# Moving the scaling of dO, the first class sorts and four short weight loads in a fused forward and backward kernel

## Chip, cores and metric

One core of one Trainium2 chip runs the whole program. The metric is the device time of one launch in microseconds; three runs of the kernel before gave 1368.88, 1370.08 and 1371.35 us, with a median of 1370.08 us. All other times come from one profiled execution, which took 1368.51 us; its span from the first to the last instruction is 1366.7 us, so 1.8 us lie around it.

## What is computed

The forward pass mixes two branches by a gate, and the program returns the output and the gradients of seven inputs:

```python
def _A_ref(x, w_r, w_i):                      # spectral branch
    X = rfft2(x.astype(float32), axes=(-2, -1)) * (w_r + 1j * w_i)
    return irfft2(X, s=(S, D)).astype(bfloat16)
def _B_ref(x, w_gate, w_up, w_down):          # GEGLU branch
    return (gelu(x @ w_gate) * (x @ w_up)) @ w_down
g = sigmoid((x * gate_w).sum(-1, keepdims=True))
out = g * _A_ref(x, ...) + (1 - g) * _B_ref(B_x, ...)
# vjp with grad_out = dO, for A_x, A_w_r, A_w_i, B_w_gate, B_w_up, B_w_down, gate_w
```

S is 2048, D is 576, F is 4608, all in bf16. The program reads the x of the GEGLU branch from A_x.

## The kernel before

**Layout.** The 2048 rows are 16 row tiles of 128. `xn` holds x and `dB` holds dO, both with rows on partitions; `xT` and `dOT` are their transposes, made on TensorE in the opening. The hidden width F is cut into 18 groups g of 256 columns.

**Steps.** The first stage (L968 to L1107) is a list of 72 steps, pr = 4g + m: group g, row tiles 4m to 4m+3. A step computes on TensorE z = dO x w_down^T (L449, L454) and xy = x x [w_gate, w_up] (L458, L465); ScalarE takes z out as `da`, scaled by 1-g (L477), and xy as `xb`, `hu` and `q` (L484 to L487); VectorE makes the derivative of the GELU in two parts, `H_ew1` (L492 to L496: four operations) and `H_ew2` (eight operations, L521 to L533, after a sigmoid on ScalarE, L512 to L516). `H_ew2` of a step, called `sigs`, is issued at the end of its step. Its results `A` and `dH` go to DRAM for the second stage, and stay on chip for the weight gradients.

**Weight gradients.** The steps of group g+1 also carry the weight-gradient jobs of group g (`W_units`): `dw` (L595, 16 matmuls of 512 columns for each of four row chunks, `w0` to `w3`) and `dwd` (L577: A^T x dB, 16 matmuls of 288 columns in two halves for each of four tiles, `d0` to `d3`). Jobs of step 5 are the halves d0 (row tiles 0 to 7), d1 (0 to 7), d0 (8 to 15) and d1 (8 to 15), in this order; they are the first that read dB as a matmul operand after the transposes. Each ends with a copy out of PSUM by ScalarE (L546). Two PSUM buffers (`wps`) serve all jobs.

**Scaling dO.** `dwd` needs (1-g) x dO. `scale_dB(k, engine)` scales row tiles 4k to 4k+3 in place, one instruction for each row tile: on ScalarE it is L964, on VectorE L966. Before the change, k = 0, 2 and 3 are ScalarE's (L1046 and L1058 in step 4, L1043 at the start of step 5) and k = 1 is VectorE's (L1063).

**The spectral branch's way in.** Between the jobs, the steps also carry pieces of the Fourier transforms (`fft`, 139 slots): for each row tile a piece u1 (L639: six matmuls, then the copy `Z` on ScalarE, L642) and a piece u2 (L653: six matmuls, then the copy `ve` on ScalarE, L659, and a chain of 16 small VectorE operations). The matmuls of u1 read `xq`, x sorted into six classes by ScalarE (`sort`, L707, one instruction for each row tile); from slot 1 on, each u1 issues one further sort. After the first three slots the order is u1, u2, u1, u2. Each piece takes the one PSUM buffer that it shares with z (pool `pz`, bufs=1). `want(pr)` says how many slots are to be done by the end of step pr: it reads `FIRST` for the first nine steps, then spreads the rest evenly up to step 64. A step's first slot goes between the two halves of its last xy, the others between jobs at even shares of their cost (L1078).

**Tables.** Step 6 runs the sines for all tables on ScalarE in one go (`run_late`, L1083), after its second job.

**Order.** The order on each engine is that of the program text; every engine takes its instructions in that order. DMAs go out by SP's queue (`LD`), by GpSimd's (`ST`) and a few by ScalarE's. In the opening, `load_w(0, 0, nc.scalar)` (L367) sends the main part of group 0's gate and up weights by SP and the last 64 rows of each, twice (partitions 0 to 63 and 64 to 127), by ScalarE's queue (L345): four DMAs of 32 KB.

The second stage (from L1110) multiplies what lies in DRAM with the weights; the change does not touch it.

Of the kernel before, what the change touches and what calls it, by code (L numbers as in the profile page):

```python
# [19 lines left out]
S, D, DF = 2048, 576, 289  # L20
# [8 lines left out]
FG = 256  # L29
# [8 lines left out]
LO, HI = slice(0, 64), slice(64, 128)  # L38
# [253 lines left out]
def kernel(  # L292
# [4 lines left out]
    nc = tc.nc  # L297
# [36 lines left out]
    def load_w(g, part, tails=LD):  # L334

        fsl = slice(g * FG, (g + 1) * FG)
        if g not in wts:
            wts[g] = (wpool.tile([P, 5, 2 * FG], BF16, tag="wgu", name="wgu"), wpool.tile([P, 5, FG], BF16, tag="wdT", name="wdT"))
        if part == 0:
            wgu = wts[g][0]  # L340
            for w, c0 in ((B_w_gate, 0), (B_w_up, FG)):
                cols = slice(c0, c0 + FG)
                LD.dma_start(wgu[:, 0:4, cols], w[0:512, fsl].rearrange("(r p) f -> p r f", p=P))
                for r in (LO, HI):
                    tails.dma_start(wgu[r, 4, cols], w[512:D, fsl])  # L345
        elif part == 1:
            LD.dma_start_transpose(wts[g][1][:, 4:5, :], B_w_down[fsl, DCH[4][0]:D])
            LD.dma_start_transpose(wts[g][1][:, 0:4, :], B_w_down[fsl, 0:512])
        else:
            LD.dma_start(wts[g][1][LO, 4, :], wts[g][1][HI, 4, :])  # L350
# [13 lines left out]
    load_do(0, 2)  # L364
    load_do(2, 2)
    load_x(0)
    load_w(0, 0, nc.scalar)  # L367
    for k in range(1, 4):
        load_do(4 * k)
        load_x(4 * k)  # L370
    tb = iotas(nc, res, unit)

    ew = wstack.enter_context(tc.tile_pool(name="ew", bufs=2))
    keepA = wstack.enter_context(tc.tile_pool(name="keepA", bufs=6))
# [552 lines left out]
    mid_at = 4 * T + 8  # L927
    NPR = NT // 2
    LASTP = NG * NPR - 7
    FIRST = (0, 0, 0, 0, 0, 0, 0, 3, 7)  # L930
    done = [0]

    def want(pr):
# [27 lines left out]
    def scale_dB(k, cp):  # L961
        for t in range(4 * k, 4 * k + 4):
            if cp == AC:
                nc.scalar.activation(dB[:, t, :], dB[:, t, :], ACT.Copy, scale=omg32[:, t:t + 1])  # L964
            else:
                V.tensor_scalar(dB[:, t, :], dB[:, t, :], omg32[:, t:t + 1], None, op0=ALU.mult)  # L966

    for g in range(NG):  # L968
        if g == 1:
            pgs.close()  # L970
            pw = ps1.enter_context(tc.tile_pool(name="pw", bufs=2, space=PSUM, **kw))
        for m in range(NPR):
            pr = g * NPR + m
            n = want(pr) - done[0]
            done[0] += n
            hs = [h for u in pend[m] for h in u] if pend else []
            inside = pend[5].get(m, []) if pend else []

            def side_work(us):
                while side and us > 0:  # L980
                    us -= side[0][0]
                    side.pop(0)[1]()
            tiles = [ewt(tag, g) for tag in ("xb", "q", "hu")]
            state = []

            def sigs(g=g, m=m, tiles=tiles, state=state):
                H_ew2(g, m, tiles, *state)
            if g == 0:
                def items(src, dst, t, *cp):
                    return titems(src, dst, 4 * t, (pgtile,) * 3, cp) if t < NPR else [None] * 3  # L990
                do1 = items(dB, dOT, 1, VC, VC, VC) if m == 0 else []
                do2 = items(dB, dOT, m + 2, AC, AC, VC)
                x1 = items(xn, xT, m + 1, AC if m else VC, VC, VC)
                z, xy_full = H_mm(g, m, [lambda: gate(0)] if m == 0 else rest, opening if m == 0 else None)
                rest = []
                da = H_da(g, m, z)
                if m == 0:
                    early, mid_, late_ = do1[:2], [do1[2], x1[0]], x1[1:]
                elif m < NPR - 1:
                    early, mid_, late_ = x1[:1], x1[1:], []  # L1000
                else:
                    early, mid_, late_ = [], [], []
                for f in early:
                    f()
                if m == 0:
                    build_R(nc, tb, unit, 0)
                xy = xy_full(0)
                for f in mid_:
                    f()
                if held and m < NPR - 1:  # L1010
                    held.pop()()
                for part in (1, 0):
                    H_act(0, xy, tiles, part)
                if held:
                    held.pop()()

                def between():
                    for f in late_:
                        f()
                xy = xy_full(1, between)  # L1020
                for part in range(2):
                    H_act(1, xy, tiles, part)
                if m == 0:
                    build_R(nc, tb, unit, 4)
                    columns_B(nc, tb, res)
                elif m == 1:
                    next(makeB)
                if m < NPR - 1:
                    gate(m + 1)
                else:  # L1030
                    V.tensor_copy(g32[:], g_bf[:])
                if m + 2 < NPR:
                    do2[0]()
                    rest = do2[1:]
                state += [*H_ew1(g, tiles, da), da]
                held.append(sigs)
            else:
                z, xy_full = H_mm(g, m)
                da = H_da(g, m, z)
                for f in inside:  # L1040
                    f()
                if pr == 5:
                    scale_dB(3, AC)  # L1043
                xy = xy_full(0)
                if held:
                    scale_dB(0, AC)  # L1046
                    held.pop()()
                k0 = int(n > 0 and pr > 6 and ready())
                xy0 = xy
                H_act(0, xy0, tiles, 1)  # L1050
                pcopy[0] = VC
                xy = xy_full(1, fft_next if k0 else None)
                pcopy[0] = AC
                H_act(0, xy0, tiles, 0)
                for part in range(2):
                    H_act(1, xy, tiles, part)
                if pr == 4:
                    scale_dB(2, AC)  # L1058
                elif pr == 6:
                    next(makeB)  # L1060
                state += [*H_ew1(g, tiles, da), da]
                if pr == 4:
                    scale_dB(1, VC)  # L1063
                    for t in range(3):
                        sort(xq, t)
                elif pr == 5:
                    build_R(nc, tb, unit, 8)
                    build_R(nc, tb, unit, 12)
                side_work(4.4)
                jobs = carry + hs  # L1070
                total = sum(w for w, _ in jobs)
                at, k, free = 0.0, k0, 0.0
                ups = upcoming(n - k0)
                last = getattr(ups[-1], "last", 0.0) if ups and (n < 5 or hasattr(ups[-1], "wide")) else 0.0
                due = [total - last - sum(getattr(u, "room", 0.9) for u in ups[j:-1]) for j in range(len(ups))]
                tables = {6: 2}.get(pr)
                for i, (w, f) in enumerate(jobs):
                    if k < n and (at >= max(min(total * k / n - 0.45, due[k - k0]), free) or len(jobs) - i <= n - k):  # L1078
                        free = at + (1.7 if wide() else 0.0)
                        fft_next()  # L1080
                        k += 1
                    if i == tables:
                        run_late(tb)  # L1083
                        wcopy[0] = VC
                    if pr == NG * NPR - 1 and at == 0.0:
                        sigs()
                    f()
                    at += w
                wcopy[0] = AC
                while k < n:  # L1090
                    fft_next()
                    k += 1
                flush()
                if pr == 6:
                    next(makeB)
                if pr < NG * NPR - 1:
                    sigs()
            carry = []
            if m < 3 and g + 1 < NG:
                for part in ((0, 1), (2,), ())[m]:  # L1100
                    load_w(g + 1, part)
            if done[0] == n_slots or (pr >= wgT_from and pr % 2 == 0 and len(wgT_all) < 20):
                load_wgT()
                if done[0] == n_slots:
                    load_wgT()
        carry = pend[4] if pend else []
        pend = W_units(g)  # L1107
# [340 lines left out]
```

## Time and profile before

| what | value |
|---|---|
| three runs, median (lowest, highest) | 1370.08 us (1368.88, 1371.35) |
| profiled execution: time / span | 1368.51 us / 1366.7 us |
| VectorE busy | 880.7 us (64%) |
| ScalarE busy | 782.4 us (57%) |
| GpSimd busy | 245.8 us (18%) |
| DMA engines' mean share, 0 to 12 us | 0.84, at 271 GB/s |
| granted TensorE clock | 1.000 |

A page of the profile lists busy time by engine, the chain that ended last, and groups of instructions by source line. "PE" is TensorE, "PEld" its weight loads, "DVE" VectorE, "ACT" ScalarE, "POOL" GpSimd. In a timeline, a row begins with the start and the length in us of a run of equal instructions, "x16" is how many there are, and the bracket at the end tells how long the engine had stood idle and what released it. The end of a matmul is modelled, so the starts are what one reckons with: 8 matmuls of 512 columns take 1.72 us from start to start of what follows (152.98 to 154.70 us), 9 of 288 columns 1.10 us (66.40 to 67.50 us).

### The profile page before, as it was taken

The numbers are of one execution on the slowest core, as the hardware profiler recorded it, in microseconds if no ns is written. First come the engines' busy times: TensorE is split into PE (matmuls) and PEld (weight loads), VectorE is DVE, ScalarE is ACT, GpSimd is POOL, SyncE is SP. The second block draws the span as 40 slices with busy tenths as digits, with TensorE's granted clock in tenths as the row PEclk, the third lists the DMA queues.
The fourth block names the chain that finished last, engine by engine and source line by source line (L and its number), as shares of the span: only waits on it lengthen the run. The fifth ranks groups of instructions, "written<-read, shape, count | busy, mean of one in ns | idle before, by whom it ended". The sixth has DMA issues, their size and how long they took to land.

```text
span 1366.7 us, 27046 instructions
## 1 busy us (share of the span) xinstructions
PE 1348.3 (99%) x10327; PEld 903.6 (66%) x10408; DVE 880.7 (64%) x2348; ACT 782.4 (57%) x1389; POOL 245.8 (18%) x484
## 2 busy tenths in 40 slices
PE   9999999999999999999999999999999999999999
PEld 7556656656656655656655655658888888888887
DVE  7888988988768876786786655525535443545320
ACT  6987888887767777776776666622332322222210
POOL 2001111111314532442441311100000000000000
PEclk9999999999999999999999999999999999999999
DMA  6424444534634644744654648499999778789773
GB/s 221 121 75 124 130 123 125 154 116 118 168 107 114 175 123 110 184 130 111 182 130 128 157 123 173 126 241 219 217 210 198 175 163 163 165 158 175 158 146 74
DMA packets 487128, 205.33 MB, mean 150 GB/s; under 512 B 306803, under 2 KB 479030, under 8 KB 486998
## 3 DMA queue, kind: packets, MB, share of 16 engines
q1 hardware_dynamic: 460660, 168.75, 53.4%
q0 software_dynamic: 14912, 24.24, 6.1%
q10 hardware_dynamic: 11426, 10.61, 3.3%
q8 instruction: 81, 1.33, 0.4%
q14 instruction: 49, 0.40, 0.1%
HBM read 41.04 MB, written 89.11 MB: 95 GB/s over the span
## 4 chain that ended last, share of the span: by engine, by line
PE 94%; ACT 3%; issue 1%; DVE 1%; DMA 0%; SPq 0%; DVEq 0%; ACTq 0%
PE acc L1198 31%; PE wps L595 17%; PE xy L465 17%; PE wps L577 10%; PE z L449 9%; PE wps L609 2%; PE xy L458 2%; PE z L454 2%; PE acc L1251 1%; PE pf L639 1%; PE acc L1261 1%; PE pf L653 1%; ACT dB L964 1%; PE pf L836 1%; PE pf L758 1%
## 5 line engine op out<-in xcount | busy, mean ns | idle before, releaser
L1198 PEld LDWEIGHTS <-pin 128*128 128x128 bf16 x3456 | 334.8, 98 | 83.2 <-issue 1.1
L465 PE MATMUL xy<-wgu,xT 128*128 128x512 bf16 x1081 | 258.0, 379 | 8.5 <-issue 7.1
L595 PE MATMUL wps<-dH,xn 128*128 128x512 bf16 x1142 | 264.4, 379 | 0.5
L595 PEld LDWEIGHTS <-xn 128*128 128x128 bf16 x1152 | 111.1, 98 | 125.0 <-issue 0.6
L465 PEld LDWEIGHTS <-xT 128*128 128x128 bf16 x1152 | 105.8, 98 | 131.9 <-issue 24.8
L602 POOL DMA_DIRECT2D out_dram<-dw x134 | 73.7, 554 | 429.5 <-ACT dw L546 411.9
L577 PE MATMUL wps<-dB,A 128*128 128x288 bf16 x1152 | 149.8, 286 | 0.5 <-ACT dw L546 0.3
L1198 PE MATMUL acc<-wd_all,pin 128*128 128x288 bf16 x1152 | 146.7, 286 | 0.0
L1198 PE MATMUL acc<-wgT,pin 128*128 128x288 bf16 x1152 | 146.6, 286 | 0.0
L1198 PE MATMUL acc<-wuT,pin 128*128 128x288 bf16 x1152 | 146.0, 286 | 0.0
L1263 ACT ACTIVATE yo<-acc 128x288 bf16<-128x288 f32 x64 | 67.4, 1246 | 133.7 <-PE acc L1261 122.3
L449 PE MATMUL z<-wdT,dOT 128*128 128x256 bf16 x1152 | 137.7, 273 | 0.6 <-ACT ve L659 0.6
L577 PEld LDWEIGHTS <-A 128*128 128x128 bf16 x1152 | 112.0, 98 | 34.1 <-issue 0.9
L477 ACT ACTIVATE da<-z,omg 128x256 bf16<-128x256 f32 x288 | 112.1, 472 | 29.6 <-PE z L454 29.5
L449 PEld LDWEIGHTS <-dOT 128*128 128x128 bf16 x1152 | 112.5, 98 | 22.2 <-issue 1.1
L1379 DVE TENSOR_TENSOR b16t<-acc,f32t 128x288 bf16<-128x288 f32 x32 | 14.6, 458 | 171.7 <-PE acc L1198 171.6
L486 ACT CAST xb<-xy 128x512 bf16<-128x512 f32 x144 | 85.1, 591 | 48.6 <-PE xy L465 48.6
L1253 ACT CAST Z<-acc 98x384 bf16<-98x384 f32 x64 | 27.5, 481 | 106.2 <-PE acc L1251 106.2
L487 ACT CAST hu<-xy 128x512 bf16<-128x512 f32 x144 | 87.4, 607 | 0.0
L484 ACT ACTIVATE q<-xy 128x512 bf16<-128x512 f32 x144 | 80.3, 601 | 3.9 <-PE xy L465 3.5
L523 DVE TENSOR_TENSOR xb<-xb,sg 128x1024 bf16<-128x1024 bf16 x48 | 33.1, 690 | 72.5 <-ACT sg L515 72.5
L546 ACT CAST dw<-wps 128x512 bf16<-128x512 f32 x72 | 42.1, 587 | 59.2 <-PE wps L595 58.6
(514 smaller groups left out, 1825.6 us busy)
## 6 DMA issues: line engine op xcount, KB each, us to landing
scr<-dH SPq DMA_DIRECT2D x144, 256.0 KB, 3.4
scr<-A SPq DMA_DIRECT2D x72, 256.0 KB, 2.4
out_dram<-dw POOLq DMA_DIRECT2D x134, 64.0 KB, 1.9
wd_all<-in_B_w_down_dram SPq DMA_DIRECT2D x3, 1728.0 KB, 13.1
out_dram<-dwd POOLq DMA_DIRECT2D x34, 144.0 KB, 3.1
scr_p<-Vt SPq DMA_DIRECT2D x32, 144.5 KB, 2.8
Vp<-scr_p ACTq DMA_DIRECT2D x32, 144.5 KB, 4.3
wgu<-in_B_w_gate_dram SPq DMA_DIRECT2D x18, 256.0 KB, 3.8
```

What stands on the lines that cost most here:

```text
L449: nc.tensor.matmul(zo(t), lhsT=dOT[:, ci, t, :], rhs=wdT[:, ci, :], start=(t % 4 < 2 and ci == 0), stop=False)
L465: nc.tensor.matmul(xy[k][:, t % 2, :], lhsT=xT[:, ci, t, :], rhs=wgu[:, ci, :], start=False, stop=(ci == 3))
L477: nc.scalar.activation(da[:, t, :], z[:, t % 2, t // 2, :], ACT.Copy, scale=omg32[:, 4 * m + t:4 * m + t + 1])
L484: nc.scalar.activation(q[:, h, :], xy[:, :, 0:FG], ACT.Square)
L486: nc.scalar.copy(xb[:, h, :], xy[:, :, 0:FG])
L487: nc.scalar.copy(hu[:, h, :], xy[:, :, FG:2 * FG])
L546: wcopy[0](out, in_)
L577: nc.tensor.matmul(wps[:, :288], lhsT=tl(0, t)[:, fch * P:(fch + 1) * P], rhs=dB[:, t, h * 288:(h + 1) * 288], start=(t == 0), stop=(t == ...
L595: nc.tensor.matmul(wps[:].rearrange("p a b -> p (a b)"), lhsT=xn[:, t, c * P:(c + 1) * P], rhs=kt[t // 4][1][:, t % 4].rearrange("p k f -> ...
L602: wst[0].dma_start(ov[:, c, fsl], dw[:, k, :])
L1198: nc.tensor.matmul(acc[:, :288], lhsT=src[:, r, :], rhs=w_of(r)[:, h * 288:(h + 1) * 288], start=(first and r == 0), stop=(last and r == F ...
L1263: nc.scalar.activation(yv[:, 3 * b:3 * b + 3], ps[:, 0:288].rearrange("p (r q) -> p r q", r=3), ACT.Copy, scale=(SD2, 1.0)[w])
```

## The change

Twelve row tiles of dO are now scaled by VectorE instead of four (k = 0 and 1 at the end of step 4, k = 3 after `H_ew1` of step 5); ScalarE keeps k = 2. The first three sorts move from the end of step 4 to one each in steps 5, 6 and 7. `FIRST` has 1 and 2 slots for steps 7 and 8 in place of 3 and 4. The four short weight loads of group 0 leave ScalarE's queue and go out by GpSimd's, after the first table indices (`iotas`).

```diff
@@ load_w
                 LD.dma_start(wgu[:, 0:4, cols], w[0:512, fsl].rearrange("(r p) f -> p r f", p=P))
-                for r in (LO, HI):
-                    tails.dma_start(wgu[r, 4, cols], w[512:D, fsl])
+                if tails:
+                    for r in (LO, HI):
+                        tails.dma_start(wgu[r, 4, cols], w[512:D, fsl])
...
-    load_w(0, 0, nc.scalar)
+    load_w(0, 0, None)
...
     tb = iotas(nc, res, unit)
+    for w, c0 in ((B_w_gate, 0), (B_w_up, FG)):
+        for r in (LO, HI):
+            ST.dma_start(wts[0][0][r, 4, c0:c0 + FG], w[512:D, 0:FG])
...
-    FIRST = (0, 0, 0, 0, 0, 0, 0, 3, 7)
+    FIRST = (0, 0, 0, 0, 0, 0, 0, 1, 3)
...
-                if pr == 5:
-                    scale_dB(3, AC)
                 xy = xy_full(0)
                 if held:
-                    scale_dB(0, AC)
                     held.pop()()
...
                 if pr == 4:
                     scale_dB(2, AC)
+                elif pr == 5:
+                    sort(xq, 0)
                 elif pr == 6:
                     next(makeB)
+                    sort(xq, 1)
+                elif pr == 7:
+                    sort(xq, 2)
                 state += [*H_ew1(g, tiles, da), da]
                 if pr == 4:
+                    scale_dB(0, VC)
                     scale_dB(1, VC)
-                    for t in range(3):
-                        sort(xq, t)
                 elif pr == 5:
+                    scale_dB(3, VC)
                     build_R(nc, tb, unit, 8)
                     build_R(nc, tb, unit, 12)
```

In the order of the instructions, three or two slots of each later step stay three or two, but every slot comes three places later from step 9 to step 30 (step 9 takes three in place of two, step 31 three in place of one) and one place later from step 31 to step 63; step 64 takes three in place of two. So a step whose three slots were u1, u2, u1 now has u2, u1, u2, and the other way round.

## Prediction

> **What bounds the kernel now.** I read the page's busy times first, then the list of TensorE's waits, then the timelines of TensorE, ScalarE and VectorE around steps 4 to 9, and last a later step that has the pattern the change will make common.
>
> ```profile
> PE 1348.3 (99%) x10327; PEld 903.6 (66%) x10408; DVE 880.7 (64%) x2348; ACT 782.4 (57%) x1389; POOL 245.8 (18%) x484
> ```
>
> TensorE stands still for 18.4 us of 1366.7. No edit removes a matmul, so only those waits can be won, or new ones made. The view of TensorE's waits (total us, times, longest):
>
> ```profile
> PE xy L465 <- issue: 7.1, 45, 0.2
> PE pf L639 <- ACT ve L659: 1.4, 1, 1.4
> PE pf L865 <- POOL ident masks.py:199: 1.4, 1, 1.4
> PE pf L420 <- DMA dB<-in_grad_out_dram: 0.9, 1, 0.9
> PE z L449 <- ACT ve L659: 0.6, 1, 0.6
> PE pf L639 <- ACT da L477: 0.5, 1, 0.5
> PE wps L577 <- ACT dw L546: 0.3, 1, 0.3
> PE wps L577 <- ACT dB L964: 0.2, 1, 0.2
> ```
>
> The 45 waits of L465 are 0.16 us each and stand where its rows count one matmul too few, so I take them for lost records. What the change can touch is ScalarE's 3.0 us (five waits, steps 5 to 8) and 0.9 us of the opening. From start to start the five are worth a little more: 0.46, 0.34, 0.64, 0.79, 1.56 us, and two of 0.14 and 0.19 beside them. Nothing from step 9 to step 71 waits.
>
> **Step 5, the scaling of dO.** VectorE's timeline (start, length):
>
> ```profile
> 59.40 1.20 DVE L966 TENSOR_SCALAR dB<-dB,omg 128x576 bf16<-128x576 bf16 x4
> 61.30 0.69 DVE L523 TENSOR_TENSOR xb<-xb,s 128x1024 bf16<-128x1024 bf16 x1 [0.70 <-ACT s L512]
> ...
> 65.63 0.69 DVE L533 TENSOR_TENSOR dH<-dH,sg 128x1024 bf16<-128x1024 bf16 x1
> 68.33 0.43 DVE L492 TENSOR_SCALAR s<-q 128x1024 bf16<-128x1024 bf16 x1 [2.01 <-ACT q L484]
> ...
> 70.41 0.69 DVE L206 CUSTOM_DVE_ANT_0 XR<-k,XR 128x1024 uint16<-128x1024 uint16 x1
> ```
>
> TensorE's:
>
> ```profile
> 59.33 3.62 PE L465 MATMUL xy<-wgu,xT 128*128 128x512 bf16 x16
> 63.25 2.98 PE L577 MATMUL wps<-dB,A 128*128 128x288 bf16 x23 [0.31 <-ACT dw L546]
> 66.40 1.26 PE L577 MATMUL wps<-dB,A 128*128 128x288 bf16 x9 [0.17 <-ACT dB L964]
> 67.50 1.91 PE L449 MATMUL z<-wdT,dOT 128*128 128x256 bf16 x16
> ```
>
> Before, ScalarE is late: three sorts (57.54, 2.7 us) and the last scaling (63.53, 2.7 us) stand in its queue. Without both, its sigmoid L512 waits only for VectorE's L493 (ends 58.54) and runs at 58.60, not 60.21; `da` and the two `dw` copies follow 1.6 us earlier. So the jobs start at 59.33 + 16 x 0.216 = 62.79, not 63.25.
>
> Now VectorE. Its scalings follow each other every 0.28 us (L966, starts 59.4 to 60.2). Eight of them end at 59.40 + 8 x 0.28 = 61.64. The `sigs` of step 4 (L523 to L533) need 66.25 - 61.30 = 4.95 us: 66.59. `H_ew1` of step 5 (L492 to the start of L206) needs 2.08: 68.67; ScalarE has its inputs ready by about 64.8. Only then come row tiles 12 to 15, done at 69.04, 69.32, 69.60 and 69.88. TensorE reaches the first matmul that reads tile 12, the 21st of the step, at 62.79 + 20 x 0.122 = 65.23. It waits until 69.09, 3.9 us, the 24th runs at 69.93, and z of step 6 starts at 69.93 + 9 x 0.122 = 71.03 instead of 67.50: **+3.5 us**, both old waits of step 5 counted as gone. Groups 0 and 1 (61.64, needed 62.79) and ScalarE's group 2 (57.68) are in time. Behind the waiting matmul stand eleven more L577, then all of step 6; ScalarE's copies of d0 and d1 wait with them.
>
> A rule speaks here. The Trainium skill ("TensorE: Matmul & The Clock Gate", Part 1: The HAM clock gate) says that TensorE falls back to half its clock after about 3.4 us of idleness, and needs as long under load to come back. No row here shows it: the longest wait after the opening is 1.4 us, and the clock row stays at 9. By that page alone an estimate would add 1.7 us.
>
> **Steps 6 and 7, one sort each.** In step 6 the sort stands on ScalarE between `hu` (76.59, the next could start at 77.07) and the copy of d2 (77.59). A sort takes 0.89 us (99.52 to 100.41), so the copy slips to 77.96, and with it the sines, the sigmoid and `da` of step 7, for which TensorE's first piece waits already (86.91). The shift by step 5 moves all of this alike. **+0.4 us.**
>
> **Steps 7 and 8, three and four slots to one and two.** The waits for `ve` (0.79, 1.56), and the two of 0.14 and 0.19 beside them, come from ScalarE's copies for pieces that are no longer there. In step 8, counted from its first piece: `ve` is out of PSUM after 0.53 + 0.70 + 0.89 + 1.90 + 0.48 + 0.65 = 5.15 us, and z of step 9 wants its buffer after 0.34 + 0.86 + 1.73 + 0.27 + 1.95 = 5.15: 0.1 left. **-2.6 us.** The four slots' matmuls (0.34 and 0.27 us each) are only put off, at no gain and no cost.
>
> **Steps 9 to 30, the pattern turned over.** A step with u1, u2, u1 was one with even m, now it has odd m. Step 12 shows how near it is:
>
> ```profile
> 149.11 0.59 ACT L486 CAST xb<-xy 128x512 bf16<-128x512 f32 x1 [0.21 <-PE xy L465]
> ...
> 153.79 0.69 ACT L659 COPY ve<-pf 128x588 f32<-128x588 f32 x1
> 154.90 0.58 ACT L546 CAST dw<-wps 128x512 bf16<-128x512 f32 x1 [0.43 <-PE wps L595]
> ```
>
> `ve` is out 5.37 us after `xb`; the second u1 takes the buffer 5.59 us after it (154.70). In steps with m = 3, w1 ends before u2, so its copy (0.48 us, 154.90 to 155.38) goes ahead of `ve`: 5.85, a wait of 0.31. Where gradients are sorted (cadence 0.97 for 0.88) it is 0.40. That is steps 11, 15, 19, 23 and 27: 2 x 0.31 + 3 x 0.40 = **+1.8 us**. With m = 1 the last u1 comes after two more halves of 288 columns and has 0.4 to spare. From step 31 on there are two slots a step; TensorE waits for none before, and I put the shift by one at nothing, covered by ScalarE's slack (bounds -0.3 to +0.5, a few waits like the above).
>
> **The opening.** The four loads take 128 KB, 0.5 us at 271 GB/s, and TensorE waits 0.87 us for dO at 7.75. By ScalarE they were issued from 1.30 to 3.78; by GpSimd, at 0.55 us each (its later stores, L602), they go out from about 1.75 to 4.0. So they still run beside dO. Best: the 0.87 goes. Worst: they land late. They took 3.4 to 6.5 us to land before, which gives 10.5 against the first use at 12.38, so a loss needs landings of over 8 us; I bound it at +1.0. I take -0.2, since the bytes due by 12.9 us stay the same. GpSimd's indices behind them end near 7 instead of 4.8 us, for a use at 14.77. The Trainium skill ("DMA: Bandwidth & Descriptors", the table at its head) puts the first byte at about 1 us for GpSimd's path and 0.6 for the others; by that an estimate adds 0.4 us to each landing, still in time.
>
> **Sum.** 3.5 + 0.4 - 2.6 + 1.8 - 0.2 = +2.9 us. The profiled execution, 1368.5, becomes 1371.4; it lies 1.6 under the median, so on the median **1373.0 us**.
>
> **Rivals.**
> - *The five waits of m = 3 stay away.* For: each rests on 0.3 us of order on ScalarE. Against: its rows agree to 0.03 us over three steps. 1371.2. Chance 0.17.
> - *VectorE is in time (not slower).* If the scaling of tile 12 ends before 65.2, because VectorE runs ahead of my chain by 3.8 us, step 5 gives -0.8 instead of +3.5: 1368.7. Against: from 57.3 to 66.3 VectorE has one gap, 0.70 us, already spent. 0.10.
> - *The wait costs speed.* After its start TensorE ran thirty 128-column matmuls in 3.38 us, where sixteen take 1.06 at 9.62: if 3.9 us of rest brings that rate back, it loses about 1.5 us once or twice: 1374.5 to 1376. 0.13.
> - *The edit in steps 7 and 8 does not do what it says:* ScalarE, after the sines, stays late, and the waits for `ve` turn up at the slots that remain: 1375.6. Against: two Z, one sort and two `ve` leave these steps, 2 x 0.70 + 0.89 + 2 x 0.55 = 3.4 us of ScalarE's time. 0.08.
> - *Short loads late:* 1374. 0.07.
>
> **Numbers.** My sum has 0.45, between 1371.8 and 1374.3. A measurement here can tell 0.2%, 2.7 us, from no change; my forecast lies just over it, at 1372.8. Slower: 0.26 + 0.02 + 0 + 0.13 + 0.08 + 0.05 = 0.54 over the cases in the order above, mine first; faster: 0.01 of the first rival, 0.05 of the second; the rest, 0.40, the same. The range 1369.5 to 1376.3 leaves out most of the second rival and a little of the top.
>
> **What would show it.** Step 5: in TensorE's waits, L577 (or its new line) released by VectorE's dB, 3 to 4 us; VectorE's last four scalings ending near 69.9 (less what the opening gave). If no such wait is there, I am wrong by 4.3 us. Steps 7 and 8: waits for `da` near 1 us, none over 0.2 for `ve`. Steps 11 to 27: five waits of 0.3 to 0.4 for `ve`, every fourth step. Clock: matmuls of 288 columns after the wait at 0.122 us; 0.24 would be the third rival. Opening: z of step 0 (8.43 before) and the first L458 (12.38).

## The result and the profile after

The change makes the kernel 0.4% slower: 1373.93 us median of 7 runs (1372.76 to 1379.08) against 1369.31 us of 7 runs of the kernel before; the ratio is 1.0043, with a 95% interval of 1.0034 to 1.0053. The profiled execution took 1372.76 us, its span is 1371.0 us, 4.3 us over that of before. The forecast for the span was +2.9 us. The profiled execution is the fastest of the seven; between the medians the change is +4.6 us.

Line numbers in the changed kernel are 4 to 6 higher (dwd's matmul is L581, its scaling on VectorE L970, z L453, `ve` L663). TensorE's waits, as in the list of before (total us, times, longest):

```profile
PE wps L581 <- DVE dB L970: 3.7, 1, 3.7
PE pf L869 <- POOL ident masks.py:199: 1.4, 1, 1.4
PE pf L643 <- ACT da L481: 0.8, 1, 0.8
PE pf L643 <- ACT ve L663: 0.7, 3, 0.2
PE acc L1204 <- ACT yo L1269: 0.6, 1, 0.6
```

ScalarE's two waits of step 5 and the two long ones for `ve` are gone, and one wait for VectorE, longer than all of them, has come. (Busy times of TensorE cannot be compared: this profile has all 10408 matmuls, the one before 10327.) VectorE's timeline around it:

```profile
59.03 2.32 DVE L970 TENSOR_SCALAR dB<-dB,omg 128x576 bf16<-128x576 bf16 x8
61.26 0.69 DVE L527 TENSOR_TENSOR xb<-xb,s 128x1024 bf16<-128x1024 bf16 x1
...
66.19 0.42 DVE L496 TENSOR_SCALAR s<-q 128x1024 bf16<-128x1024 bf16 x1
...
68.26 1.20 DVE L970 TENSOR_SCALAR dB<-dB,omg 128x576 bf16<-128x576 bf16 x4
```

TensorE's:

```profile
68.67 3.16 PE L581 MATMUL wps<-dB,A 128*128 128x288 bf16 x12 [3.65 <-DVE dB L970]
71.63 2.07 PE L453 MATMUL z<-wdT,dOT 128*128 128x256 bf16 x16
```

VectorE does the twelve row tiles as reckoned, and tile 12 is ready at 68.6 us (forecast 69.04, less the 0.4 that the opening gave). But from the first matmul after the wait to z there are 2.96 us, not 1.94. The table of stretches tells why (length, TensorE's busy time and matmuls, granted clock, DMA share, GB/s):

```profile
62.40:65.00 2.60, 2.60 (x21) 1.00 0.63 152
65.00:68.60 3.60, 0.02 (x1) 0.99 0.94 267
68.60:70.00 1.40, 1.33 (x6) 0.50 0.18 45
70.00:72.00 2.00, 2.00 (x10) 0.52 0.03 8
72.00:74.00 2.00, 2.00 (x22) 1.00 0.18 71
```

After the rest TensorE runs at half clock for 3.4 us: its first matmuls come every 0.28 us, as VectorE's tiles do, and the later ones every 0.24 us instead of 0.122.

**The lag, step by step.** The best view for a change in a kernel that one engine bounds is made of the starts of z in each step, after minus before (from the timelines):

| start of z of step | lag, us | what lies between |
|---|---|---|
| 1 to 5 | -0.38 | the opening |
| 6 | +4.13 | +4.50: wait for tile 12, half clock |
| 7 | +4.28 | +0.16: the last of the half clock |
| 8 | +3.13 | -1.15: `da` 0.4 later, `ve` 0.9 less, two slots put off (0.6) |
| 9 | +0.78 | -2.34: 1.7 of waits gone, two slots put off (0.6) |
| 10 | +1.12 | +0.33: one slot made up |
| 12, 16, 20, 24, 28 | 1.43, 1.73, 2.13, 2.51, 2.90 | +0.36, +0.36, +0.46, +0.45, +0.45 across steps 11, 15, 19, 23, 27 |
| 31 | +3.78 | +0.9: three slots made up |
| 71 | +3.78 | nothing more in the first stage (from 32 to 64 it is +3.53: one slot put off, then made up) |

The last half microsecond is a wait of the second stage (the list's fifth line), which no other run here shows; nothing here ties it to the change.

### The profile page after: what moved, and what is told of

Its sections match the earlier page's. It is cut to its first block, busy times and chain, and to the rows that moved or that the text cites. A ratio compares the mean times of both kernels' runs of the same rounds, so it can differ in the third digit from the quotient of the medians.

```text
span 1371.0 us, 27120 instructions
## 1 busy us (share of the span) xinstructions
PE 1359.5 (99%) x10408; PEld 904.6 (66%) x10408; DVE 881.8 (64%) x2355; ACT 776.8 (57%) x1382; POOL 244.7 (18%) x488
## 4 chain that ended last, share of the span: by engine, by line
PE 94%; DVE 2%; ACT 2%; DMA 1%; issue 0%; POOL 0%; ACTq 0%; DVEq 0%; POOLq 0%
PE acc L1204 30%; PE xy L469 18%; PE wps L599 17%; PE wps L581 10%; PE z L453 9%; PE wps L613 2%; PE xy L462 2%; PE z L458 2%; PE pf L643 1%; PE acc L1257 1%; PE pf L840 1%; PE acc L1267 1%; PE pf L762 1%; DMA pin<-scr 1%; PE pf L657 1%; PE pf L408 0%
## 5 line engine op out<-in xcount | busy, mean ns | idle before, releaser
L469 PE MATMUL xy<-wgu,xT 128*128 128x512 bf16 x1152 | 270.5, 380 | 0.0
L581 PE MATMUL wps<-dB,A 128*128 128x288 bf16 x1152 | 151.6, 287 | 3.7 <-DVE dB L970 3.7
L453 PE MATMUL z<-wdT,dOT 128*128 128x256 bf16 x1152 | 137.9, 273 | 0.1
L581 PEld LDWEIGHTS <-A 128*128 128x128 bf16 x1152 | 112.2, 98 | 37.6 <-issue 4.4
L453 PEld LDWEIGHTS <-dOT 128*128 128x128 bf16 x1152 | 112.6, 98 | 21.8 <-DVE dOT L425 0.3
```

The costliest lines, as they stand in the source:

```text
L453: nc.tensor.matmul(zo(t), lhsT=dOT[:, ci, t, :], rhs=wdT[:, ci, :], start=(t % 4 < 2 and ci == 0), stop=False)
L469: nc.tensor.matmul(xy[k][:, t % 2, :], lhsT=xT[:, ci, t, :], rhs=wgu[:, ci, :], start=False, stop=(ci == 3))
L581: nc.tensor.matmul(wps[:, :288], lhsT=tl(0, t)[:, fch * P:(fch + 1) * P], rhs=dB[:, t, h * 288:(h + 1) * 288], start=(t == 0), stop=(t == ...
```

## The experiments

Each compares with the first profile of the kernel before, by the same view of lags; "edit" is against the changed kernel unless said otherwise. Only e1 and e5 ran more than once. The others are one execution each, so of them the growth of the lag within the execution is read rather than the whole time.

### All scalings of VectorE in step 4 (e1_tiles12_step4)

```diff
                     scale_dB(0, VC)
                     scale_dB(1, VC)
+                    scale_dB(3, VC)
                 elif pr == 5:
-                    scale_dB(3, VC)
                     build_R(nc, tb, unit, 8)
```

> The changed kernel, with the last four scalings of dO moved on VectorE from step 5 (behind the sigs of step 4 and H_ew1 of step 5) to the end of step 4, behind the other eight. My theory: the place in VectorE's queue is what makes TensorE wait 3.65 us, and the wait in turn costs about 1 us of half clock. The twelve scalings end by 59.03 + 12 x 0.28 = 62.4 us, tile 12 is needed at 64.9: no wait, clock share 1.00 throughout, z of step 6 at 62.41 + 32 x 0.122 = 66.3 instead of 71.63, and the start of the last step's z 1.7 us before that of the kernel before (it was 3.8 us after it). Span 1365 us give or take the half microsecond of the second stage; faster than before by 0.1%. Rival: VectorE is simply too full in steps 4 and 5, so the wait comes back elsewhere (for the sigmoid, da or a copy of step 6): z of step 7 gains under 3 us.

Measured: 1366.97 us against 1367.97 (10 and 13 runs), ratio 0.9991 (0.9981 to 1.0001); span 1365.0 us. Its VectorE and TensorE:

```profile
59.19 3.43 DVE L970 TENSOR_SCALAR dB<-dB,omg 128x576 bf16<-128x576 bf16 x12
62.54 0.68 DVE L527 TENSOR_TENSOR xb<-xb,s 128x1024 bf16<-128x1024 bf16 x1
```

```profile
62.57 4.08 PE L581 MATMUL wps<-dB,A 128*128 128x288 bf16 x32
66.49 1.91 PE L453 MATMUL z<-wdT,dOT 128*128 128x256 bf16 x16
```

All 32 matmuls in one piece; the clock is 1.00 in every stretch; z of step 7 is 1.01 us ahead of before instead of 4.28 behind, the last step's 1.45 ahead. The last four scalings, on the same engine and 6.8 us earlier (from 61.42 us instead of 68.26), make no wait. So it is the place in VectorE's queue, not VectorE's load; the rival falls.

### The part alone (e7_scalings_alone)

Edit, against the kernel before: only the scalings move, as in the change; sorts, slots and loads stay.

> The kernel before, with nothing but the scalings moved as the change moves them (eight by VectorE in step 4, four in step 5 behind H_ew1); sorts, slots and loads as before. My theory: this edit alone carries the loss: a wait of 3 to 3.7 us for VectorE at dO's tile 12, half clock after it for about 3.4 us if the rest is long enough, lag of 4.3 to 4.7 us from step 6 on, kept to the last step since the waits of steps 7 and 8 (0.5, 0.6, 1.4 us) are still there. Rival: the three sorts, which still stand ahead of the sigmoid on ScalarE, delay VectorE too, and the wait is over 4.5 us.

Measured: span 1371.5 us. From step 5 to step 7 the lag grows by 5.86 us and then stays, +4.80 at every later step to the last.

```profile
PE wps L577 <- DVE dB L966: 3.2, 1, 3.2
PE pf L639 <- ACT ve L659: 1.4, 1, 1.4
...
PE z L449 <- ACT ve L659: 0.6, 1, 0.6
PE pf L639 <- ACT da L477: 0.5, 1, 0.5
```

This one edit carries the loss; the waits of steps 7 and 8 are as before, so what removed them is the slots or the sorts, which stay here; no run parts these two. The wait is as expected (3.2 us, since 0.3 of the old wait for a `dw` copy goes ahead of it), but the growth is over the 4.3 to 4.7 that I expected: here the half clock lasts 6.83 us, not 3.41. The table of stretches, as above:

```profile
62.40:65.00 2.60, 2.44 (x20) 1.00 0.69 166
65.00:68.60 3.60, 0.61 (x3) 0.76 0.87 254
68.60:70.00 1.40, 1.40 (x8) 0.50 0.06 12
70.00:72.00 2.00, 2.00 (x10) 0.50 0.00 0
72.00:74.00 2.00, 2.00 (x12) 0.57 0.19 74
```

A mean of 0.76 from 65.0 to 68.6 us puts the fall near 66.9 us, about 2.1 us into the rest, which runs from 64.84 to 67.99 us by the modelled matmul ends.

### The wait filled (e3_wait_filled, e8_wait_filled_a_little)

```diff
                 for t in range(8 * half, 8 * half + 8):
+                    if g == 0 and (fch, h, t) == (0, 0, 12):
+                        keep_on = pftile()
+                        for _ in range(56):   # 8 in the second kernel
+                            nc.tensor.matmul(keep_on[:, 0, :P], lhsT=ident[:], rhs=ident[:], start=True, stop=True)
                     nc.tensor.matmul(wps[:, :288], ...
```

> The changed kernel, with 56 matmuls of 128 columns on the identity, into a PSUM buffer that nobody reads, before the matmul that waits for dO's tile 12 (56 x 0.056 = 3.1 us of the 3.65). The wait for VectorE stays, only TensorE is kept at work. My theory: the granted clock falls to half because TensorE rested; at work it stays at 1.00, the eight matmuls behind the wait take 0.122 us each, z of step 6 starts at about 70.5 instead of 71.63, and the lag at step 7 is 1.1 to 1.2 us smaller (about 3.1 instead of 4.28). Rival: the matmuls after the wait are slow because VectorE or the semaphores pace them: z of step 6 stays at 71.6.

> As the kernel with the filled wait, but with 8 matmuls of 128 columns instead of 56, so that TensorE rests about 3.2 us instead of 3.65. If the rest must be as long as the stretch that the clock took to come up in the opening (3.4 us), the share stays at 1.00 and the lag at step 7, counted from step 5, is 3.5 us as with 56; if it needs less, it falls to 0.50 as in the changed kernel, and the lag grows by 4.6 us.

Measured, 56 matmuls:

```profile
66.74 3.29 PE L584 MATMUL pf<-ident 128*128 128x128 bf16 x56
70.56 2.10 PE L585 MATMUL wps<-dB,A 128*128 128x288 bf16 x12 [0.52 <-DVE dB L974]
72.49 1.69 PE L453 MATMUL z<-wdT,dOT 128*128 128x256 bf16 x14
```

From the first matmul after VectorE to z it is 1.93 us, as reckoned without a clock in it, and the clock stays at 1.00. The absolute times are 1.9 us later than expected, because this execution lost 1.5 us in its opening (below); from step 5 to step 7 the lag grows by 3.48 us, against 4.65 in the changed kernel. So the wait costs 3.48 and the half clock 1.17 us. Work that nobody needs makes the kernel faster there; in the whole it does not show, for the span is 1371.0 us, as in the changed kernel, after the slower opening.

Measured, 8 matmuls:

```profile
64.21 0.61 PE L584 MATMUL pf<-ident 128*128 128x128 bf16 x8
68.02 3.16 PE L585 MATMUL wps<-dB,A 128*128 128x288 bf16 x12 [3.19 <-DVE dB L974]
70.97 3.29 PE L453 MATMUL z<-wdT,dOT 128*128 128x256 bf16 x16
```

A rest of 3.19 us is enough for the clock to fall (again 2.1 us after its start), and z too runs at half speed (3.29 us for 1.91): the fall lasts 6.83 us, from step 5 to step 7 the lag grows by 5.87 us, of which 2.39 are the clock's. I had expected 3.5 or 4.6; the second half of the "if" was right and its size too small. (The 3.4 us in it are not what the opening shows: in the first profile of before the clock came up 4.5 us after the first matmul, 1.37 to 5.90 us.)

### The last four scalings one place earlier (e6_tiles12_before_ew1)

Edit: `scale_dB(3, VC)` of step 5 stands before `H_ew1`.

> The changed kernel, with the last four scalings ahead of H_ew1 of step 5 instead of behind it. My theory: tile 12 is done at 66.19 + 0.37 = 66.56 us instead of 68.6, TensorE waits 1.5 us from 65.0, too short a rest to lose the clock: share 1.00, z of step 6 at 67.4 + 9 x 0.122 = 68.5 us; lag at step 7 about 1.0 us instead of 4.28, span near 1367.8. Rival: any wait at this place costs clock, in proportion: share under 0.9 after the wait, lag over 1.5 us.

Measured: span 1367.8 us.

```profile
67.33 2.10 PE L581 MATMUL wps<-dB,A 128*128 128x288 bf16 x12 [1.57 <-DVE dB L970]
69.27 1.91 PE L453 MATMUL z<-wdT,dOT 128*128 128x256 bf16 x16
```

A rest of 1.57 us here costs no clock (share 1.00, 1.94 us to z). z of step 6 is 0.7 us later than expected, as is everything from step 1 on in this execution (lag +0.37 at step 5); so the lag of +1.77 at step 7, over the 1.5 named for the rival, is no sign of it: from step 5 to step 7 the lag grows by 1.40.

### The slots turned back (e2_slots_1_3_5)

```diff
-    FIRST = (0, 0, 0, 0, 0, 0, 0, 1, 3)
+    FIRST = (0, 0, 0, 0, 0, 0, 0, 1, 3, 5)
```

> The changed kernel, with two slots in step 9 (FIRST ends in 1, 3, 5), so that the steps with three slots have u1, u2, u1 at even m again, as in the kernel before. My theory: the five growths of the lag at steps 11, 15, 19, 23 and 27 (0.3, 0.3, 0.4, 0.4, 0.4 us) come from the copy of w1 that stands ahead of ve, and go: TensorE's waits for ve vanish from the list, lag behind the kernel before at the last step's z 3.78 - 1.8 = 2.0 us, span about 1369.2 us (or 1368.7, if the 0.56 us wait of the second stage is chance). Rival: they come from ScalarE being late after the new order of steps 4 to 8, and stay at even m: lag 3.8 us.

Measured: span 1368.4 us; the lag is +0.70 at step 10 and +0.70 at step 28, and 1.92 at the last step. TensorE has no wait for `ve` left:

```profile
PE wps L581 <- DVE dB L970: 3.7, 1, 3.7
PE pf L869 <- POOL ident masks.py:199: 1.4, 1, 1.4
PE pf L643 <- ACT da L481: 0.9, 1, 0.9
PE acc L1195 <- ACT dw L550: 0.5, 1, 0.5
PE pf L408 <- DVE dOT L415: 0.2, 1, 0.2
```

The mechanism is seen in step 11 of the changed kernel, ScalarE and then TensorE:

```profile
138.04 0.58 ACT L490 CAST xb<-xy 128x512 bf16<-128x512 f32 x1 [0.69 <-PE xy L469]
...
142.72 0.63 ACT L550 CAST dw<-wps 128x512 bf16<-128x512 f32 x1
143.19 0.70 ACT L663 COPY ve<-pf 128x588 f32<-128x588 f32 x1
```

```profile
141.91 1.89 PE L599 MATMUL wps<-dH,xn 128*128 128x512 bf16 x8
143.94 0.50 PE L643 MATMUL pf<-Rt,xq 128*96 128x128 bf16 x6
```

The copy of w1 stands ahead of `ve`, which ends 5.85 us after `xb`, the figure of the forecast to the hundredth; the u1 starts 5.90 after it, 2.03 us after the eight matmuls instead of 1.72. This wait fell between two rows that the modelled matmul ends nearly close: the rows show only 0.14 to 0.24 us of each 0.30 to 0.40, and the list of waits names three.

### Both mends together (e5_both_mended)

> The changed kernel with both mends together: all twelve scalings of VectorE at the end of step 4, and slots 1, 3, 5 for the ends of steps 7, 8, 9. My theory: the two costs are independent, so the gains add. Span 1365.0 - 1.8 = 1363.2 us, about 1365.0 us in time, 0.25% under the kernel before (3.2 to 3.5 us). Rival: with the waits of step 5 gone ScalarE is nearer to TensorE, and the mend of the slots gives less than 1 us.

Measured: 1364.94 us (11 runs) against 1368.00 (15 runs), ratio 0.9978 (0.9969 to 0.9987), span 1363.0 us. Lag -1.23 at step 6, -4.69 from step 9 to step 28 (1.2 of it slots put off), -3.47 at the end. The gains add, and this version is faster than both kernels. What ScalarE was freed of was worth 3 us; the change spent it twice over.

### The opening (e4_loads_alone, e12_loads_alone_again, e13_before_again)

Edit, against the kernel before: only the four short loads go by GpSimd's queue; the last is the kernel before, unchanged.

> The kernel before, with nothing but the four short weight loads moved to GpSimd's queue. My theory: the 0.37 us by which the changed kernel leads up to step 5 is this edit's alone (dO's second piece lands before TensorE asks for it): z of step 1 at 19.28, all later steps 0.37 us ahead of the kernel before up to the last, span 1366.3. Rival: the lead came from the reordered first steps of ScalarE and VectorE and is not there by step 1.

> The kernel before with the four short loads by GpSimd, a second profile. The kernel with the scalings alone, which leaves the loads to ScalarE, led the first profile by 1.05 us at step 1, and kernels with GpSimd's loads stand between -1.03 and +1.50 there. Theory: the opening varies by about a microsecond from one execution to the next, in the landing of dO's second piece; z of step 1 is anywhere from 18.6 to 21, so the edit's own worth cannot be told from the scatter. Rival: again about 0.3 us ahead of the first profile of the kernel before.

> The kernel before, unchanged, for a second profile of its opening. Theory: z of step 1 is not at 19.66 again but anywhere from 18.6 to 21; from step 1 to the last step's z the two profiles agree within 0.05 us. Rival: the kernel before is steady (19.6 to 19.7), and GpSimd's loads are worth 0.3 to 0.4 us.

Measured, lag at the start of z of step 1 (all in us; it stays within 0.1 of this to step 5 in each run):

| loads | lag in each profile |
|---|---|
| by ScalarE | 0 (first profile of before), -0.49 (e13), -1.05 (e7) |
| by GpSimd | -0.38 (changed), -0.23 (e1), -0.45 (e2), +1.50 (e3), -0.28 (e4), -0.43 (e5), +0.36 (e6), -1.03 (e8), +1.55 (e12) |

The first of the three seemed to settle it: the loads alone gave -0.28 and kept it to the end (span 1366.3). The next kernels threw that over, and the two repeats agree: the same kernel stands at -0.28 and +1.55, and the kernel before at 0 and -0.49. The opening scatters by more than the loads can be worth, and what they are worth stays open; the theory that the lead is theirs falls.

In e3 and e12 the +1.5 has a reason that can be seen. In e12:

```profile
5.89 0.62 PE L424 MATMUL pf<-ident,dB 128*128 128x128 bf16 x8
7.75 0.78 PE L424 MATMUL pf<-ident,dB 128*128 128x128 bf16 x8 [1.24 <-DMA dB<-in_grad_out_dram]
...
8.75 1.91 PE L453 MATMUL z<-wdT,dOT 128*128 128x256 bf16 x8
```

The eight matmuls of z take 1.91 us for 1.04 before: TensorE fell back to half clock (share 0.57 from 8 to 12 us) after a wait of 1.24 us for dO.

## Why the prediction was right, and where it was off

- *What bounds:* right. Every microsecond of the result is a wait of TensorE or its clock.
- *Step 5:* right. Forecast +3.5 us by a wait of 3.9; the wait is 3.65 plus what the modelled ends hide, and with the clock kept up it costs 3.48 us (e3). The chain was VectorE's own order: eight scalings, `sigs`, `H_ew1`, then tile 12.
- *The clock:* **the step that failed.** I gave "the wait costs speed" 0.13, and the sum held no term for it. It came in every one of the four kernels with a rest of 3.15 us or more, and cost 1.17 us in the changed kernel's profile and 2.4 us in e7 and e8; the rival's 1.5 once or twice was near. Of the 4.3 us of the span it is the largest part that I left out. The Trainium skill ("TensorE: Matmul & The Clock Gate", Part 1: The HAM clock gate) had the right warning: half clock after about 3.4 us of idleness, and a window of activity to come back. The trace agrees on the 0.50 and on the 3.41 us. The rest needed was shorter here: in e7 and e8 the clock fell 2.1 us into it. I weighed the rule against rows that held no long wait, and those could not speak against it; nor could the profile's clock row, which stays at 9 in the changed kernel too, since a slice there is 34 us long.
- *Steps 6 and 7:* right. TensorE's wait for `da` grew from 0.46 to 0.85 us, +0.4 as forecast, with the sort on ScalarE ahead of the copy of d2 (81.35 and 82.24 us); no run moves that sort alone.
- *Steps 7 and 8:* right. -2.6 forecast; together with the 0.4, the lag falls by 3.49 us from step 7 to step 9, of which 1.22 are four slots put off: -2.27 against -2.2.
- *Five waits at m = 3:* right, place and size. 0.30 us for each of the first two and 0.40 for the other three, net of the slots' turns, +1.8 as forecast; the slots turned back take 1.86 away (e2).
- *From step 31 on:* right, nothing.
- *The opening:* -0.2 forecast, -0.38 in the profile, but no run can say that the loads did it. The four loads landed 4.9 to 6.8 us after their issue (median 5.6), against 3.4 to 6.5 (median 6.3) in the profile of before, and TensorE waited for neither; the 0.4 us more for each landing is not seen in these medians.
- *The sum:* +2.9 became +4.3: 1.17 for the clock and 0.56 for one wait of the second stage, less 0.3 of roundings. By these terms the span without the clock would have been +3.1. That the forecast time, 1373.0 us, lies within 1 us of the measured median is in part luck: it started from a median of 1370.08 us where seven runs give 1369.31.
- The seven runs spread from 1372.8 to 1379.1 us, and their mean granted clock is 0.997 to 0.999, where the kernel before has 1.000 in all but two of its runs (0.999). Part of the spread is likely to be one or two windows of half clock (3.41 or 6.83 us, both seen); that it explains the slowest run is not shown.

## What to carry to other kernels

When work moves to an engine that is "off the critical path", follow the queue of that engine to the place where the work is now issued, and set its end against the matmul that needs it: the share of busy time (64% here) says nothing of it. Where TensorE bounds a kernel, price a wait of over 2 us at more than its length: here half clock came 2.1 us into a rest and cost 1.2 to 2.4 us more, while a rest of 1.57 us, or matmuls to nowhere, kept the clock. And write down the start of the same instruction in every step, before and after: that table showed four separate causes, of 0.3 to 4.5 us, that the total hides.

## What I had not expected of the hardware

- TensorE lost its clock in rests of 3.15 (e7), 3.19 (e8) and 3.65 us (the changed kernel, e2) and kept it in rests of 1.57 (e6) and, filled, 0.52 us (e3). The time at half clock came as 3.41 or 6.83 us, never between.
- The clock records of the traces change only in steps of 3.413 us. In these four kernels the fall comes 61.44 us, 18 such steps, after the rise in the opening: 7.08 to 68.52 us in the changed kernel, 6.93 to 68.37 in e2, 5.47 to 66.91 in e7, 5.52 to 66.96 in e8. (The rise shows in the matmuls of 128 columns too, which come every 0.107 us before it and every 0.056 after.) In the changed kernel and e2 the fall lies at the end of the rest, TensorE works nearly all of the next step, and one step runs at half clock. In e7 and e8 the fall lies inside the rest, over 1 us of the next step is still rest, and it takes two. So the cost of a wait goes by where it lies in these steps as well as by its length; since no run moved the one without the other, how much is due to each stays open.
- In the opening 1.24 us were enough (e12; 1.30 in e3), although 1.19 in e6 and 0.85 in e1 were not. The fall came one step after the rise (4.65 to 8.06 us in e12). Why less than e6's later 1.57 us was enough is not shown.
- SP's own DMAs went out earlier when ScalarE issued none: its third load of dO at 3.73 to 4.38 us in the nine profiles with GpSimd's loads, at 5.14 to 5.58 in the three with ScalarE's. Its last load of x overlaps between the two (8.13 to 9.72 against 9.54 to 10.84). No gain for TensorE could be told from it.
